# Gated mix of attention and a spectral filter on one core: values as weights of four heads, part of the exponentials as bit patterns on two other engines, folded transforms, an order planned ahead

## The chip, the cores and the metric

One core of a Trainium2 chip runs the kernel. The time is the device time of one execution in microseconds (us); a version's time is the median of its runs. Engines: PE (TensorE: matmuls; PEld is its weight load), DVE (VectorE), ACT (ScalarE), POOL (GpSimd), SP (SyncE, which here issues nearly all DMAs). Each engine works through its own row of instructions in order and waits on semaphores for the others.

## The reference

`x` is 1 x 2048 x 448. A gate of one number per token mixes two branches: softmax attention with 16 heads of width 28, and a filter in the two-dimensional Fourier domain.

```python
g = sigmoid((x * gate_w).sum(-1, keepdims=True))
q, k, v = split(x @ wqkv)                     # 16 heads, Dh = 28
p = softmax(einsum("bhqd,bhkd->bhqk", q, k) * Dh ** -0.5)
a = heads_joined(einsum("bhqk,bhkd->bhqd", p, v)) @ wo
b = irfft2(rfft2(x) * (w_r + 1j * w_i))       # over tokens and features
return g * a + (1 - g) * b
```

There are 16 x 2048 x 2048 exponentials, 1024 blocks of 128 keys by 512 queries of one head.

## The kernel before, in words

*Set-up.* `phase_setup` loads the tokens (`xtok`) and transposes them on PE into `xT`. `proj_setup` and `proj_matmuls` build, for up to four heads at a time, `qTa` and `kTa`: 32 rows for each head, 28 of them data and one a norm that keeps the exponent in range (`proj_knorm` and the bias function behind it: squares, sums by a matmul, a maximum, a DMA that puts the row in place). `vproj_and_gate` makes the values `vsb` (28 columns and a column of ones) and the gate.

*Main loop.* `main_loop_group` goes over six groups: one head by itself, then five groups of three heads. For each block of 512 queries and each of 16 blocks of 128 keys it issues three score matmuls into three PSUM banks (`psS`, two such tiles; each head uses its own 32 rows of the array, so that three run side by side), one exponential on ACT over all three banks (128 x 1536, L557), and 12 value matmuls (L562): there the exponential `Pt` is the weight, in pieces of 128 x 128, and `vsb` (29 columns) streams past it. The result has queries on partitions; DVE divides it by the column of sums (L568, L571).

*Background.* The projections of later heads and the transforms are issued at a low priority between the steps; a scheduler orders all engines by that. They share one PSUM bank (`ps_bg`). The transforms are `fft_f1` (over features), `fft_f2` (over tokens, 128 points), `fft_f34` (transposes, 16-point step with twiddles, product with the filter), `fft_f5` and `fft_f678` (the way back, ending in `bm_sb`, already multiplied by 1 - g). The `tail` transposes each token block of the attention result, multiplies by `wo` and adds `bm_sb`.

Of the kernel before, what the change touches and what calls it, by code (L numbers as in the profile page):

```python
# [12 lines left out]
F32 = mybir.dt.float32  # L13
ACT = mybir.ActivationFunctionType
# [3 lines left out]
BG_PRIORITY_BASE = 10_000_000  # L18


def bcast_last(ap: bass.AP, n: int) -> bass.AP:
    assert ap.ap[-1][1] == 1
    new_ap = [list(p) for p in ap.ap[:-1]] + [[0, n]]
    return bass.AP(tensor=ap.tensor, offset=ap.offset, ap=new_ap)


def strided_rows(t_ap: bass.AP, row0: int, stride: int, count: int) -> bass.AP:
    pstep = t_ap.ap[0][0]
    return _AP(tensor=t_ap.tensor, offset=t_ap.offset + row0 * pstep,
               ap=[[pstep * stride, count]] + [list(x) for x in t_ap.ap[1:]])  # L30


def chunks_of(n: int, c: int):
    return [(i, min(c, n - i)) for i in range(0, n, c)]


def fft_consts(S: int, D: int):
    NT = S // 128
    P = 128
    J = P // NT  # L40
    F = D // 2 + 1
    F2 = 2 * F
    bf16 = ml_dtypes.bfloat16
    fch = chunks_of(F, 128)
    c = {}
    d = np.arange(D)[:, None]
    f = np.arange(F)[None, :]
    Bd = np.concatenate([np.cos(2 * np.pi * d * f / D), -np.sin(2 * np.pi * d * f / D)], axis=1)
    dch = chunks_of(D, 128)
    Bd_pad = np.zeros((len(dch) * 128, F2))  # L50
    Bd_pad[:D] = Bd
    c["Bd"] = np.ascontiguousarray(Bd_pad.reshape(len(dch), 128, F2).transpose(1, 0, 2))
    pp = np.arange(P)[:, None]
    bb = np.arange(P)[None, :]
    Ec = np.cos(2 * np.pi * pp * bb / P)
    Es = np.sin(2 * np.pi * pp * bb / P)
    def perm(M):
        return np.ascontiguousarray(M.reshape(P, J, NT).transpose(0, 2, 1).reshape(P, P))
    R = np.zeros((P, 4, 256))
    R[:, 0, :] = np.concatenate([perm(Ec), perm(-Es)], axis=1)  # L60
    R[:, 1, :] = np.concatenate([perm(Es), perm(Ec)], axis=1)
    R[:, 2, :] = np.concatenate([perm(Ec), perm(Es)], axis=1)
    R[:, 3, :] = np.concatenate([perm(-Es), perm(Ec)], axis=1)
    c["R"] = R
    CS = np.zeros((NT, P, 3, P))
    tt = np.arange(NT)[:, None]
    aa = np.arange(NT)[None, :]
    for g in range(NT):
        for j in range(J):
            b = g + NT * j  # L70
            th = 2 * np.pi * (tt * aa / NT + tt * b / S)
            CS[g, j::J, 0, j::J] = np.cos(th)
            CS[g, j::J, 1, j::J] = np.sin(th)
            CS[g, j::J, 2, j::J] = -np.sin(th)
    c["CS"] = CS
    RB = np.zeros((NT, P, 2, 2 * P))
    for g2 in range(NT):
        for j2 in range(J):
            bh = g2 + NT * j2
            ps = 2 * np.pi * (tt * aa / NT + tt * bh / S)  # L80
            RB[g2, j2::J, 0, j2:P:J] = np.cos(ps)
            RB[g2, j2::J, 0, P + j2::J] = np.sin(ps)
            RB[g2, j2::J, 1, j2:P:J] = -np.sin(ps)
            RB[g2, j2::J, 1, P + j2::J] = np.cos(ps)
    c["RB"] = RB
    mm = np.arange(D)[None, :]
    ff = np.arange(F)[:, None]
    cfac = np.full((F, 1), 2.0)
    cfac[0, 0] = 1.0
    cfac[F - 1, 0] = 1.0  # L90
    Br = cfac * np.cos(2 * np.pi * ff * mm / D) / (S * D)
    Bi = -cfac * np.sin(2 * np.pi * ff * mm / D) / (S * D)
    Binv = np.zeros((P, 2 * len(fch), D))
    qi = 0
    for B in (Br, Bi):
        for (fs, fn) in fch:
            Binv[:fn, qi, :] = B[fs:fs + fn, :]
            qi += 1
    c["Binv"] = Binv
    return {k: v.astype(np.float32).astype(bf16) for k, v in c.items()}  # L100


class Kernel:
    def __init__(self, tc, A_x, A_wqkv, A_wo, B_w_r, B_w_i, gate_w, out):
        self.tc = tc
        nc = self.nc = tc.nc
        self.A_x, self.A_wqkv, self.A_wo = A_x, A_wqkv, A_wo
        self.B_w_r, self.B_w_i, self.gate_w, self.out_ap = B_w_r, B_w_i, gate_w, out
        self.H = H = 16
        self.S = S = A_x.shape[1]  # L110
        self.D = D = A_x.shape[2]
        self.Dh = Dh = D // H
        self.SCALE = float(Dh) ** -0.5
        self.NT = NT = S // 128
        self.P = P = 128
        self.J = P // NT
        self.F = F = D // 2 + 1
        self.F2 = 2 * F
        self.dch = chunks_of(D, 128)
        self.NDC = len(self.dch)  # L120
        self.fch = chunks_of(F, 128)
        self.QW = 512
        assert Dh + 1 <= 32 and S % 512 == 0 and P % NT == 0 and NT <= P and H % 4 == 0
        self.x = A_x[0]
        self.outv = out[0].rearrange("(p t) d -> p t d", t=NT)
        self.tiles = [[(s, 4 * T + s) for s in range(4)] for T in range(H // 4)]
        lastT = len(self.tiles) - 1
        hl = H - 1
        self.tiles[lastT] = [(s, h) for (s, h) in self.tiles[lastT] if h != hl]
        self.tiles.append([(0, hl)])  # L130
        self.repT = len(self.tiles) - 1
        self.head_loc = {}
        for T, ent in enumerate(self.tiles[:-1]):
            for s, h in ent:
                self.head_loc[h] = (T, s)
        groups = [("rep", hl)]
        others = [h for h in range(H) if h != hl]
        for i in range(0, len(others), 3):
            groups.append(("tri", others[i:i + 3]))
        self.groups = groups  # L140
        self.NG = len(groups)
        self._bgcount = 0
        self._bg_saved = None
        self._evac_cnt = 0

    def bg_begin(self):
        assert self._bg_saved is None
        self._bg_saved = self.tc.cur_priority
        self.tc.cur_priority = BG_PRIORITY_BASE + self._bgcount

    def bg_end(self):
        assert self._bg_saved is not None
        self._bgcount = self.tc.cur_priority - BG_PRIORITY_BASE
        self.tc.cur_priority = self._bg_saved
        self._bg_saved = None

    def setup_pools(self, ctx):
        tc = self.tc
        self.per = ctx.enter_context(tc.tile_pool(name="per", bufs=1))
        self.rot2 = ctx.enter_context(tc.tile_pool(name="rot2", bufs=2))  # L160
        self.rot3 = ctx.enter_context(tc.tile_pool(name="rot3", bufs=3))
        self.ps = ctx.enter_context(tc.tile_pool(name="ps", bufs=2, space=bass.MemoryType.PSUM))

    def ps_S(self, shape, dt, name):
        return self.ps.tile(shape, dt, name=name, tag="psS", bufs=2)

    def ps_pv(self, shape, dt, name):
        return self.ps.tile(shape, dt, name=name, tag="pv", bufs=1)

    def ps_bg(self, shape, dt, name):  # L170
        return self.ps.tile(shape, dt, name=name, tag="bg", bufs=1)

    def evac2(self, o, i):
        if self._evac_cnt % 2 == 0:
            self.nc.vector.tensor_copy(out=o, in_=i)
        else:
            self.nc.scalar.copy(out=o, in_=i)
        self._evac_cnt += 1

    def build(self):  # L180
        with ExitStack() as ctx:
            self.setup_pools(ctx)
            self.phase_setup()
            self.fft_setup()
            NTL = len(self.tiles)
            self.qTt = [None] * NTL
            self.kTt = [None] * NTL
            def full_proj(Tlist):
                for T in Tlist:
                    self.proj_setup(T)  # L190
                for which in ("q", "k"):
                    for T in Tlist:
                        self.proj_matmuls(T, which)
                for T in Tlist:
                    self.proj_knorm(T)
                for T in Tlist:
                    self.proj_qbias(T)
            full_proj([self.repT, 0])
            self.vproj_and_gate()
            bg_items = [("proj", T) for T in range(1, NTL - 1)]  # L200
            bg_items += [("fft", f) for f in
                         [self.fft_f1, self.fft_f2, self.fft_f34, self.fft_f5, self.fft_f678]]
            npj = NTL - 2
            plan = {0: [0, npj], 1: [1, npj + 1], 2: [2, npj + 2], 3: [npj + 3], 4: [npj + 4]}
# [99 lines left out]
    def proj_setup(self, T):  # L304
# [4 lines left out]
        if not hasattr(self, "Waug"):  # L309
            self.Waug = {}  # L310
            self._wc = 0
# [489 lines left out]
```

## Time and profile before

| | us |
|---|---|
| median of 2 runs (584.65 to 585.45) | 585.05 |
| span of the profiled execution | 564.9 |
| PE busy in it | 508.8 |
| ACT busy in it | 490.0 |
| DVE busy in it | 213.8 |
| POOL busy in it | 20.8 |

The page gives the span of the profiled execution, from its first to its last instruction, and no other time of its own for it. The two runs lie 20.2 us above that span: what lies around the instructions. PE's busy time is modelled and takes in waiting inside the pipeline, so a busy PE isn't PE at its peak. The granted clock of PE is given in every window; 1.00 is full speed.

### The profile page before, as it was taken

To read this page: it belongs to the slowest core of one execution; us is meant where nothing else is said; L and a number is where in the kernel's file an instruction comes from. 1 tells how busy PE (TensorE), PEld (TensorE's weight loads), DVE (VectorE), ACT (ScalarE), POOL (GpSimd) and SP (SyncE) were. 2 spreads that over 40 slices of the span, in tenths; PEclk is the share of its full clock that TensorE was granted. 3 is DMA by queue.
4 is the path that set the end of the run, shared out by engine and by line. 5 is a ranking of instruction groups with operands and counts; after the bars stand their busy time and mean duration, and the time that the engine had idled before them with its cause. 6 is when DMAs were issued, how large, how long until landed. Compare 5 with 4: busy or idle time off the path is not lost.

```text
span 564.9 us, 13975 instructions
## 1 busy us (share of the span) xinstructions
PE 508.8 (90%) x6088; PEld 256.5 (45%) x6088; DVE 213.8 (38%) x633; ACT 490.0 (87%) x392; POOL 20.8 (4%) x92
## 2 busy tenths in 40 slices
PE   2979988999998899999899999999998998899986
PEld 2424432444443355544355555555544554445541
DVE  4573323322223533322556555333233233333343
ACT  2153986999999899999899999999999999999961
POOL 6240010000000000000000000000000000000000
PEclk9989985699999575799575555757799589999996
DMA  7300000000000000000012221000000000000111
GB/s 252 126 19 20 2 2 1 2 1 2 2 1 2 3 1 1 1 3 1 1 33 54 55 55 26 1 2 1 20 21 20 21 20 20 21 1 27 34 34 41
DMA packets 13947, 13.45 MB, mean 24 GB/s; under 512 B 6191, under 2 KB 12783, under 8 KB 13758
## 3 DMA queue, kind: packets, MB, share of 16 engines
q1 hardware_dynamic: 13886, 12.57, 7.8%
q8 instruction: 47, 0.77, 0.6%
q14 instruction: 14, 0.11, 0.1%
HBM read 10.14 MB, written 1.84 MB: 21 GB/s over the span
## 4 chain that ended last, share of the span: by engine, by line
ACT 48%; PE 39%; issue 7%; DVE 3%; DMA 1%; SPq 0%; ACTq 0%
ACT Pt L557 48%; PE psS L553 12%; PE psPV L562 9%; PE pv L290 2%; PE pqk L353 2%; PE psT L641 2%; DMA Wqkv_sb<-in_A_wqkv_dram 1%; PE psY L714 1%; PE pf_s L747 1%; PE ptx L257 1%; PE psB L662 1%; PE psA L623 1%; PE psZ L705 1%; DVE fin L749 1%; PE psB L664 1%
## 5 line engine op out<-in xcount | busy, mean ns | idle before, releaser
L557 ACT ACTIVATE Pt<-psS 128x1536 bf16<-128x1536 f32 (+1 forms) x352 | 469.4, 1460 | 19.4 <-PE psS L553 10.2
L562 PEld LDWEIGHTS <-Pt 128*128 128x128 bf16 x4096 | 142.3, 100 | 131.1 <-ACT Pt L557 109.6
L562 PE MATMUL psPV<-vsb,Pt 128*128 128x29 bf16 x4096 | 167.1, 182 | 25.3 <-ACT Pt L557 20.8
L553 PE MATMUL psS<-qTa_2343,kTa_2344 32*128 32x512 bf16 x256 | 69.3, 507 | 0.5 <-ACT Pt L557 0.5
L553 PE MATMUL psS<-qTa_950,kTa_951 32*128 32x512 bf16 x256 | 68.8, 530 | 0.4 <-ACT Pt L557 0.4
L553 PE MATMUL psS<-qTa_249,kTa_250 32*128 32x512 bf16 x256 | 60.6, 439 | 1.8 <-ACT Pt L557 1.8
L553 PE MATMUL psS<-qTa_3760,kTa_3761 32*128 32x512 bf16 x192 | 26.5, 384 | 0.5 <-ACT Pt L557 0.4
L718 DVE TENSOR_SCALAR bm_sb<-psY,omg 128x448 bf16<-128x448 f32 x16 | 10.9, 683 | 36.8 <-PE psY L714 36.8
L667 DVE CAST Xri<-psB 128x225 bf16<-128x225 f32 x16 | 6.3, 396 | 25.7 <-PE psB L665 25.7
L749 DVE SCALAR_TENSOR_TENSOR fin<-pf,gsb,bm_sb 128x448 bf16<-128x448 f32 x12 | 8.2, 684 | 20.7 <-PE pf L747 20.7
L257 PE MATMUL ptx<-ident,xtok 128*128 128x128 bf16 (+1 forms) x64 | 6.7, 287 | 10.3 <-DMA xtok<-in_A_x_dram 7.7
L553 PEld LDWEIGHTS <-kTa_250 32*128 32x128 bf16 x256 | 12.8, 93 | 6.4 <-issue 2.3
L747 PE MATMUL pf<-Wo_sb,oTt 128*128 128x448 bf16 (+1 forms) x48 | 14.8, 374 | 0.7 <-DVE oTt L740 0.7
L553 PE MATMUL psS<-qTa_207,kTa_208 32*128 32x512 bf16 x64 | 14.4, 420 | 0.6 <-ACT Pt L557 0.5
L553 PEld LDWEIGHTS <-kTa_951 32*128 32x128 bf16 x256 | 13.0, 97 | 4.1 <-issue 1.8
L553 PEld LDWEIGHTS <-kTa_2344 32*128 32x128 bf16 x256 | 13.0, 95 | 3.6 <-issue 1.2
L571 DVE TENSOR_TENSOR osb<-psPV,recip 128x112 bf16<-128x112 f32 x64 | 13.6, 266 | 0.6
L290 PE MATMUL pv<-Wqkv_sb,xT 128*128 128x449 bf16 x64 | 13.5, 372 | 0.0
L603 DVE CAST V_5523<-psA 97x256 bf16<-97x256 f32 x16 | 6.8, 424 | 16.4 <-PE psA L625 16.4
L603 DVE CAST U_192<-psA 128x256 bf16<-128x256 f32 x16 | 6.8, 425 | 15.7 <-PE psA L625 15.7
L623 PE MATMUL psA<-R_sb,X_sb 128*128 128x256 bf16 (+1 forms) x32 | 12.2, 383 | 0.0
L623 PE MATMUL psA<-R_sb,G_sb 128*128 128x256 bf16 (+1 forms) x32 | 12.2, 382 | 0.0
(484 smaller groups left out, 541.6 us busy)
## 6 DMA issues: line engine op xcount, KB each, us to landing
RBg<-cRB SPq DMA_DIRECT2D x16, 128.0 KB, 2.0
xtok<-in_A_x_dram SPq DMA_DIRECT2D x1, 1792.0 KB
out_dram<-fin SPq DMA_DIRECT2D x16, 112.0 KB, 1.7
CSg<-cCS SPq DMA_DIRECT2D x16, 96.0 KB, 1.8
Wqkv_sb<-in_A_wqkv_dram SPq DMA_DIRECT2D x3, 336.0 KB, 7.4
Wg<-in_B_w_r_dram SPq DMA_DIRECT2D x16, 56.2 KB, 1.8
Wg<-in_B_w_i_dram SPq DMA_DIRECT2D x16, 56.2 KB, 2.0
Bd_sb<-cBd SPq DMA_DIRECT2D x1, 450.0 KB, 3.8
```

Source lines behind the costliest of these rows:

```text
L257: nc.tensor.transpose(out=pt[0:dsz, k, :], in_=self.xtok[:, t, d0:d0 + dsz], identity=self.ident[:])
L290: nc.tensor.matmul(pv[:, e, 0:D + 1], lhsT=self.xT[:, c, 128 * t:128 * t + 128], rhs=self.Wqkv_sb[:, c, 2 * D:3 * D + 1], start=(c == 0), ...
L353: nc.tensor.matmul(pqk[0:M, e, :], lhsT=Wg[:, c, 0:M], rhs=self.xT[:, c, 512 * b:512 * b + 512], start=(c == 0), stop=(c == NDC - 1))
L553: nc.tensor.matmul(psS[:, e, :], lhsT=kTa[32 * s:32 * s + 32, 128 * i:128 * i + 128], rhs=qTa[32 * s:32 * s + 32, qs:qs + QW], start=True, ...
L557: nc.scalar.activation(out=Pt[:, 0:ne, :], in_=psS[:, 0:ne, :], func=ACT.Exp, scale=self.SCALE)
L562: nc.tensor.matmul(psPV[:, e, j, 0:Dh + 1], lhsT=Pt[:, e, 128 * j:128 * j + 128], rhs=self.vsb[:, i, h, 0:Dh + 1], start=first, stop=last)
L571: nc.vector.tensor_tensor(out=self.osb[:, t0:t0 + NQT, h * Dh:(h + 1) * Dh], in0=psPV[:, e, :, 0:Dh], in1=bcast_last(recip[:, e, :, 0:1], Dh),
L603: self.nc.vector.tensor_copy(out=o, in_=i)
L623: nc.tensor.matmul(ps[0:fn, :], lhsT=data_sb[:, t, fs:fs + fn], rhs=Rr, start=True, stop=False)
L641: nc.tensor.transpose(out=psT[:, ri * 256 + fs:ri * 256 + fs + fn], in_=U_tiles[fb][0:fn, ri, g, :], identity=self.ident[0:fn, 0:fn])
L747: nc.tensor.matmul(pf[:, 0:D], lhsT=oTt[0:dsz, c, :], rhs=self.Wo_sb[0:dsz, c, :], start=(c == 0), stop=(c == NDC - 1))
L749: nc.vector.scalar_tensor_tensor(out=fin[:], in0=pf[:, 0:D], scalar=self.gsb[:, t:t + 1], in1=self.bm_sb[:, t, :], op0=ALU.mult, op1=ALU.add)
```

## The change

The kernel is written anew; only the arithmetic of the reference is common. Part by part:

*Values as weights.* `Wp` pads each head to 32 columns, so four heads stand in 128 rows of `qT` and `kT`. The values `V` (32 columns for each head: 28 data, one weight, three zeros) are now the weight of a matmul and 512 exponentials stream past it. The four heads use the four groups of 32 columns of the array and write the four 32-row parts of one bank `pv`. A chunk is four heads by 512 queries: 16 chunks instead of the 21 of before.

*Exponentials in three places.* `stream` takes the 1024 blocks in steps. In each of 360 steps two blocks go to ACT (128 x 1024, `PA`), and in 304 of them a third goes to DVE: scores are scaled so that a score plus a constant, clamped at zero and written as a 16-bit integer, is the bit pattern of a bf16 number near the exponential. GpSimd makes two shifted copies of the pattern (two blocks at once where it can), and PE adds all three copies with weights `W2` and `W3` in the values `V[1]`, `V[2]`: such a block costs three value matmuls, one on ACT costs one.

```diff
+nc.scalar.activation(out=s_ap[:, 0:len(pk)], in_=bank[:, 0:len(pk), :], func=ACT.Exp, scale=LN2 / 128.0)
...
+nc.vector.tensor_scalar(out=tl[:, 0, e, :], in0=self.single[b][:], scalar1=C2, scalar2=0.0,
+                        op0=ALU.add, op1=ALU.max)
...
+for j, sh in ((1, N2), (2, N3)):
+    nc.gpsimd.tensor_scalar(out=t[:, j, 0:n, :], in0=t[:, 0, 0:n, :], scalar1=float(sh), scalar2=1.0,
+                            op0=ALU.add, op1=ALU.mult)
...
+def score(self, out, g, c, i, h):
+    r = slice(32 * h, 32 * h + 30)
+    self.mm(out, self.kT[g % 2][r, 128 * i:128 * i + 128], self.qT[self.chunks.index((g, c)) % 3][r, :],
+            pos=(32 * h, 0))
...
+self.mm(self.pv[32 * h:32 * h + 32, :], self.V[g % 2][e["j"]][:, i, h, :], e["ap"],
+        start=f, stop=False, pos=(0, 32 * h))
-nc.scalar.activation(out=Pt[:, 0:ne, :], in_=psS[:, 0:ne, :], func=ACT.Exp, scale=self.SCALE)
...
-nc.tensor.matmul(psPV[:, e, j, 0:Dh + 1], lhsT=Pt[:, e, 128 * j:128 * j + 128],
-                 rhs=self.vsb[:, i, h, 0:Dh + 1], start=first, stop=last)
```

*Division.* `normalise` copies `pv` (DVE), sends the four rows of sums through DRAM and back in another layout (DMAs on SP), takes reciprocals times the gate, spreads them through DRAM to 32 rows each, and multiplies: `oT`, already transposed. The last chunk does it on DVE alone with 32 x 32 transposes. The output then needs no transpose and no gate.

*Folded transforms.* `e_f1_pe` takes features d and 448 - d together (`xr` is the mirrored copy, made by GpSimd), `e_f2_pe` uses cosine and sine halves, `e_f3_pe` and `e_f3_t` do twiddles and filter, `e_f5_pe` and `e_f6_pe` go back; the last step over tokens and the factor 1 - g (`Rg`, `Rn`) are matmuls that add into the same bank as `oT @ wo` (`e_o_pe`). The filter comes in 16 groups of frequencies, each with 18 DMAs (16 of them rows of `w_r` and `w_i`).

```diff
+def e_f3_t(self, b, bg, r):
+    o = (self.T1, self.T2)[r][bg % 2]
+    self.nc.vector.tensor_tensor(out=o[:], in0=b[:, 0:450].rearrange("p (r f) -> p r f", r=2),
+                                 in1=bc_at(self.Wf[bg % 2][:, r, :], 1, 2), op=ALU.mult)
...
+def e_o_pe(self, b, t):
+    for g in range(4):
+        self.mm(b[:, 0:448], self.oT[:, g, 128 * t:128 * t + 128], self.Wo[:, g, :], start=g == 0, stop=False)
+    self.mm(b[:, 0:225], rp, eo[:, 0:225], start=False, stop=False)
...
```

*Order.* A `Planner` places every task on its engine by assumed durations and writes all rows in that order, with no scheduler behind it (`tc.manual_schedule()`). Scores wait for one of two ACT banks (`pair`) or three single banks (`single`, shared with all background work); value matmuls are taken in groups of up to eight. Two of its rules:

```diff
+n_dve = 310
+unit(f"F2_{bg}", t0, [("PE", 0.55, self.e_f2_pe, (bg,)), ("DVE", 0.56, self.e_f2_ev, (bg,))],
```

PE's row before, late in the main loop, at the end of one value group, one step of scores, and a piece of transform:

```order
L562 LDWEIGHTS Pt_6371
L562 MATMUL psPV_6240<-vsb_172,Pt_6371 128x29
L553 LDWEIGHTS kTa2_2344
L553 MATMUL psS_6403<-qTa2_2343,kTa2_2344 128x512
L553 LDWEIGHTS kTa2_2344
L553 MATMUL psS_6403<-qTa2_2343,kTa2_2344 128x512
L553 LDWEIGHTS kTa2_2344
L553 MATMUL psS_6403<-qTa2_2343,kTa2_2344 128x512
L705 LDWEIGHTS VT_6934
L705 MATMUL psZ_6948<-RBg_6932,VT_6934 97x256
```

Exponentials (`Pt`) were weights and 29 columns streamed. PE's row now, in a chunk of the second group of heads (`PA` and `PD` are exponentials of ACT and DVE, `pair` and `one` score banks):

```order
L328 LDWEIGHTS V1_0_77
L328 MATMUL pv_145<-PD0_136,V1_0_77 32x512
L328 LDWEIGHTS V1_0_77
L328 MATMUL pv_145<-PA1_130,V1_0_77 32x512
L328 LDWEIGHTS V1_0_77
L328 MATMUL pv_145<-PA1_130,V1_0_77 32x512
L328 LDWEIGHTS kT1_73
L328 MATMUL pair0_140<-qT1_70,kT1_73 128x512
L328 LDWEIGHTS kT1_73
L328 MATMUL pair0_140<-qT1_70,kT1_73 128x512
L328 LDWEIGHTS kT1_73
L328 MATMUL one2_144<-qT1_70,kT1_73 128x512
```

The values are the weight, 512 columns stream, and PE goes from column tiles to row tiles with each step. Over the whole program PE has 291 runs of score matmuls, 218 runs of value matmuls and 133 runs of matmuls over the full array.

DVE's row before, in the filter stage of the transforms:

```order
L667 CAST Xri_4178<-psB_4173 128x225
L668 CAST Xri_4178<-psB_4173 128x225
L673 TENSOR_TENSOR cm_t1_4181<-Xri_4178,Wg_4162 128x225
L674 TENSOR_TENSOR cm_t2_4182<-Xri_4178,Wg_4162 128x225
L678 TENSOR_TENSOR cm_t1_4186<-Xri_4178,Wg_4162 128x225
```

Now, in the same stage, DVE's row holds patterns (`PD`) at nearly every second place, between transforms (`Z`), the division (`oT`) and the gate (`xr`):

```order
L903 TENSOR_SCALAR PD3_139<-one0_142 128x512
L903 TENSOR_SCALAR PD3_139<-one1_143 128x512
L660 TENSOR_TENSOR xr_64<-one2_144,cR_85 128x512
L903 TENSOR_SCALAR PD0_136<-one0_142 128x512
L903 TENSOR_SCALAR PD0_136<-one1_143 128x512
L903 TENSOR_SCALAR PD1_137<-one0_142 128x512
L742 CAST Z_81<-one1_143 113x64x8
L903 TENSOR_SCALAR PD1_137<-one0_142 128x512
```

A late transform or division now stands in front of the patterns on DVE, and the patterns in front of GpSimd's copies and PE's value matmuls.

More of the change, by code (lines that the diff above doesn't have):

```diff
@@ L6 @@
 from concourse.bass_types import AP as _AP
-from concourse.masks import make_identity
 import concourse.tile as tile
-from concourse import bass_utils
 from concourse._compat import with_exitstack
@@ new lines, with __init__, placed, done @@
+class Task:
+    __slots__ = ("eng", "dur", "fn", "deps", "start", "end", "done", "seq", "land", "key", "mode", "placed", "then", "port")
+    def __init__(self, eng, dur, fn, deps=(), land=0.0, key=0.0, mode=None, then=None, port=False):
+        self.eng, self.dur, self.fn, self.deps = eng, dur, fn, [d for d in deps if d is not None]
+        self.land, self.key, self.mode, self.then, self.port = land, key, mode, then, port
+        self.placed = False
+class Unit:
+    def __init__(self, name, target, phases, deps=(), bank=True):
+        self.name, self.target, self.phases, self.deps, self.bank = name, target, phases, list(deps), bank
+        self.tasks = []
+        self.opened = False
+    @property
+    def placed(self):
+        return self.opened and len(self.tasks) == len(self.phases) and self.tasks[-1].placed
+    @property
+    def done(self):
+        return max(t.done for t in self.tasks)
+    @property
+    def eng(self):
+        return self.tasks[-1].eng
@@ L768 @@
 ):
[L769 to L770 removed]
+    with tc.manual_schedule():
+        Kernel(ctx, tc, A_x, A_wqkv, A_wo, B_w_r, B_w_i, gate_w, out).build()
 _INS = ['A_x', 'A_wqkv', 'A_wo', 'B_x', 'B_w_r', 'B_w_i', 'gate_w']
```

1647 lines of the change are left out of this document (956 added, 691 removed).

## The prediction

> **What bounds the kernel now.** I read the page first: busy times, granted clock, and the chain that ended last.
>
> ```profile
> PE 508.8 (90%) x6088; PEld 256.5 (45%) x6088; DVE 213.8 (38%) x633; ACT 490.0 (87%) x392; POOL 20.8 (4%) x92
> PEclk9989985699999575799575555757799589999996
> ACT 48%; PE 39%; issue 7%; DVE 3%; DMA 1%; SPq 0%; ACTq 0%
> ```
>
> ACT and PE share the chain; DVE and POOL have room. The clock row has stretches at half speed. Then busy times by windows of 40 us (columns: length, PE, PEld, DVE, ACT, POOL with counts, granted clock, DMA share, GB/s), and the groups by shape.
>
> ```profile
> 140.00:180.00 40.00, 36.96 (x500) 17.21 (x497) 8.74 (x16) 40.00 (x31) 0.00 (x0) 1.00 0.01 2
> 180.00:220.00 40.00, 35.94 (x434) 17.96 (x433) 17.69 (x40) 35.90 (x27) 0.00 (x0) 0.64 0.01 2
> 300.00:340.00 40.00, 39.04 (x486) 22.90 (x486) 23.09 (x108) 37.56 (x28) 0.00 (x0) 0.50 0.23 55
> L557 ACT ACTIVATE Pt<-psS 128x1536 bf16<-128x1536 f32 x336 | 460.2, 1500 | 16.4 <-PE psPV L562 7.9 <-PE psS L553 7.5 <-PE pn_3826 L493 0.4
> L557 ACT ACTIVATE Pt<-psS 128x512 bf16<-128x512 f32 x16 | 9.6, 609 | 2.9 <-PE psS L553 2.7 <-PE psPV L562 0.2
> L562 PE MATMUL psPV<-vsb,Pt 128*128 128x29 bf16 x4096 | 167.1, 182 | 25.3 <-ACT Pt L557 20.8
> L562 PEld LDWEIGHTS <-Pt 128*128 128x128 bf16 x4096 | 142.3, 100 | 131.1 <-ACT Pt L557 109.6 <-issue 6.9 <-DVE osb L571 3.8
> ```
>
> In the main loop ACT is busy for all 40 us of a quiet window and 35.90 where background work crowds PE and DVE: the exponentials bound the middle, and mixing in work costs the bounding engine 10.25% there. Outside the middle:
>
> ```profile
> PE ptx L257 <- DMA xtok<-in_A_x_dram: 7.7, 1, 7.7
> 56.81 4.13 ACT L557 ACTIVATE Pt<-psS 128x1536 bf16<-128x1536 f32 x3 [0.23 <-PE psS L553]
> 543.77 1.61 ACT Pt L557
> 559.70 1.78 PE pf_s L747 x4
> ```
>
> The first exponential starts at 56.8 us, the last ends near 545, the span at 564.9: 78 us lie outside the loop.
>
> **The change, part by part.** One third of the blocks leaves ACT, so I price all engines and look for the longest.
>
> *ACT.* Pitch, not duration, counts, because rows overlap:
>
> ```profile
> 80.66 1.11 ACT L557 ACTIVATE Pt<-psS 128x512 bf16<-128x512 f32 x2 [0.23 <-PE psPV L562]
> 511.64 6.87 ACT L557 ACTIVATE Pt<-psS 128x1536 bf16<-128x1536 f32 x5
> ```
>
> Five of 1536 in 6.87 with a last one of 1.50 give (6.87 - 1.50)/4 = 1.34 us; two of 512 give 1.11 - 0.60 = 0.51. Between them 0.81 ns an element, so 1024 elements take 0.925. ACT has 360 of these (333 us) and 34 of 512 (squares of the projections, output copies: 17): with a few small ones 351 us, where it had 490.
>
> *PE.* Prices at full clock:
>
> ```profile
> 21.60 2.76 PE L353 MATMUL pqk<-xT,WaugQ_209 128*128 128x512 bf16 x12
> 47.77 7.59 PE L290 MATMUL pv<-Wqkv_sb,xT 128*128 128x449 bf16 x39
> 512.24 0.39 PE L553 MATMUL psS<-qTa_3760,kTa_3761 32*128 32x512 bf16 x3
> 512.57 0.66 PE L747 MATMUL pf<-Wo_sb,oTt 128*128 128x448 bf16 x2
> ```
>
> Twelve matmuls of 512 columns: (2.76 - 0.38)/11 = 0.216 us each. Thirty-nine of 449: (7.59 - 0.37)/38 = 0.190. So 0.413 ns a column and 4.6 ns a matmul. Three score matmuls side by side start at 512.24 and the next work at 512.57: 0.33, of which 0.216 is one turn and 0.11 the change to other tiles.
>
> - Scores: 1024 still, each in its 32 rows. In the program they make 355 turns (a turn is one matmul in each row group that has one) in 291 runs: 355 x 0.216 + 291 x 0.11 = 109 us.
> - Values: 4096 weight loads with 29 columns go; 1632 matmuls of 512 columns come (720 blocks once, 304 blocks three times). The trace shows no column tiles. Bound below: four at once, as the score rows run three at once, with the program's unevenness 543 turns in 218 runs: 543 x 0.216 + 218 x 0.11 = 141. Bound above: one after another, 1636 x 0.216 + 24 = 377. I take 141, because the score row is the same array split the other way and shows full overlap.
> - Full array (projections, values, transforms, output): 1145 matmuls, 260,896 columns, 133 runs: 5.3 + 107.7 + 14.6 = 128. The folding is in this count; the transposes of the old transforms and of the old tail are gone.
>
> PE: 378 us. This is the longest row, though its busy time of before can't be set against it, since that takes in waiting.
>
> *DVE.* Start to start of a 512-column read from PSUM:
>
> ```profile
> 56.27 0.69 DVE L478 CAST qTa_950<-pqk_952 128x512 bf16<-128x512 f32 x1
> 56.88 0.16 DVE L298 TENSOR_SCALAR ge<-ge 128x16 f32<-128x16 f32 x1
> ```
>
> 0.61 us. DVE has 496 instructions of about this size (304 patterns, 192 for projections, values, transforms, division, output): 303 us; 22 of 1024 elements at some 0.65 and 90 small ones at 0.15 add 28: 331 us, 54% more than before, but under PE.
>
> *GpSimd.* It gets 296 shifts of 1024 elements and 16 of 512; no such instruction is in the trace. The nearest rows:
>
> ```profile
> L458 POOL COPY WaugK_905<-Wqkv_sb 128x28 bf16<-128x28 bf16 x12 | 2.0, 208 | 0.1
> masks.py:199 POOL TENSOR_SCALAR_AFFINE_SELECT ident<-ident 128x128 bf16<-128x128 bf16 x1 | 0.3, 292 | 0.1
> L265 POOL MEMSET xT<- 64x2048 bf16 x1 | 1.8, 1804 | 0.1
> L316 POOL MEMSET WaugQ_209<- 128x512 bf16 x1 | 0.5, 534 | 0.0
> ```
>
> The two that read and write 16-bit data give (292 - 208)/100 = 0.84 ns an element, so 1.05 us for 1024 and 0.61 for 512: 320 us. If the fixed part is the memsets' (534 less 512 at their slope of 0.83 ns, 0.11 us), AFFINE_SELECT says (292 - 110)/128 = 1.42 ns and the sum is 296 x 1.56 + 16 x 0.84 = 475. I take 320, since copy and select share the way an instruction reads. Trainium skill, "GPSIMD Engine Reference", 3.1: 1.03 cycles an element for at most two operations, 1.8 in the tight loops measured there; at the 1.2 GHz it gives, I estimate 0.86 or 1.5 ns. The first agrees with 0.84, the second is near 1.42; no run here shows which holds for integers.
>
> *SP.* Issue and landing:
>
> ```profile
> 320.10 0.33 SPq L655 DMA_DIRECT2D CSg<-cCS  x1
> 44.19 0.65 SPq L421 DMA_DIRECT2D qTa_249<-brow  x1
> Wg<-in_B_w_r_dram SPq DMA_DIRECT2D x16, 56.2 KB, 1.8
> ```
>
> SP goes from some 100 DMAs to 440: 288 for the filter groups, 105 for 15 divisions, 47 others; at 0.33 us 145 us. I cost it at nothing: a division has the length of a chunk (some 25 us) before its buffer is needed, against four hops of 1.8 and their issue; a filter group has a second buffer. If that cover is gone, DVE stands in front of the filter product, with the patterns queued behind it, then GpSimd's copies, then PE's value matmuls: rival D.
>
> **Sum.** PE starts behind the tokens (7.7 us before) and has little work in the chain of square, norm and copy of the first projection (0.5 + 0.6 us each, a few links): 12 us. Projection, gate and norms of later heads run inside the loop, so the 56.8 us go. After the last value matmul come five DVE instructions, four output blocks in a pipeline of copy and 1.8 us store: 10 us, half of before. In the middle PE, DVE, ACT and GpSimd all have 85 to 100% of PE's load and hand blocks over through two ACT banks, three shared banks and four pattern buffers; the bounding engine then loses what ACT lost in 180 to 220 us, so 378/0.8975 = 421. Span 12 + 421 + 10 = 443. The runs lie 20.2 us over the profiled span (585.05 against 564.9), so 463 us.
>
> **The rivals.**
>
> *A, the column tiles don't run at once* (slower). Value matmuls one after another: PE 614, /0.8975 = 684, with 22 and 20 it is 726 us. It decides from the point where PE's sum is (585 - 42) x 0.8975 = 487, the value term 250, which is fewer than 1.56 of four at once (1632 x 0.216/226). For it: no row shows column tiles. Against it: the score row.
>
> *F, they overlap in part.* A value turn costs 0.27 instead of 0.216, halfway to the 0.33 of a score turn with its change: 543 x 0.27 + 24 = 171, PE 408, 455 + 42 = 497 us. For it: eight matmuls read eight different streams of exponentials, where score rows share a width of 32. Trainium skill, "TensorE: Matmul & The Clock Gate", Part 3, gives three column tiles of 512 columns a gain of 2.38, not 3, which would be 117/0.79 = 148 for the turns, by my estimate the same as 543 x 0.27; no run here shows it yet.
>
> *B, half clock.* The trace shows when it falls and rises:
>
> ```profile
> 36.00:40.00 4.00, 3.24 (x9) 0.65 (x9) 3.17 (x5) 1.06 (x2) 2.34 (x12) 0.65 0.00 0
> 40.00:44.00 4.00, 4.00 (x11) 0.86 (x10) 0.34 (x3) 3.53 (x4) 0.00 (x0) 0.50 0.01 1
> 44.00:48.00 4.00, 4.00 (x23) 2.01 (x22) 1.62 (x2) 0.38 (x2) 0.00 (x0) 0.99 0.33 70
> ```
>
> It falls after a gap in PE's work and returns with dense matmuls; in 300 to 340 us it stayed at 0.50 with short waits in between. At the mean of before, 0.805, the streaming part of PE's sum (898 turns and 113 us, 307) becomes 381, the sum 452, and the time 504 + 42 = 546 us. Under 0.74 it would be slower than before. Against it: PE is nearly full now, and the quiet loop held 1.00 with less work.
>
> *C, GpSimd bounds.* At 1.42 ns: 475, with some 25 us before its first copies and 15 behind its last 515, and 535 us; at the same loss as PE more, about 555. For it: the memset reading above.
>
> *D, a late filter takes the place of the wait on exponentials.* If each of 16 groups comes half its issue time (18 x 0.33/2 = 3.0 us) late: 48 us, 511 us. For it: SP's row is in order and divisions stand between the groups. The same price covers other handovers that are worse than 10%.
>
> *E, no loss.* PE without gaps: 378 + 22 + 20 = 420 us; ACT's own floor is 351 + 42 = 393.
>
> That the change doesn't do what it says is excluded by the counts of its rows: 304 of 1024 blocks leave ACT, 30%.
>
> **Chances.** Forecast (435 to 485) 0.47, A 0.05, F 0.09, B 0.13, C 0.08, D 0.08, E 0.10. The predicted time is the forecast's, 463. The range 418 to 552 takes in E, F, D and most of B, and leaves out A, most of C and the upper end of B, under 0.2. A measurement of this kernel tells about 2% from no change. A and the low end of B's clocks are slower, 0.06; C with more loss or B near its turning point could come within 2%, 0.03; the rest is faster, 0.91.
>
> **What would show it.** The scores: three at once at a pitch of 0.33. The value groups: eight matmuls in 0.54 us (right), 0.65 (F) or 1.7 (A). GpSimd's shift of 1024: 1.05 us or 1.6. ACT busy 351, first exponential before 20 us. Clock above 0.9. DVE waiting on DMAs before T would show D. The prediction is wrong if PE isn't the longest row, or if its gaps in the middle are far from 10%.

## The result, and the profile after

The kernel became slower: 644.66 us (642.72 to 646.60, 2 runs) against 585.05, a ratio of 1.101 (95%: 1.093 to 1.110). Forecast were 463 us. The runs of the kernel before fall in two groups, 562 to 574 and 581 to 588 us; 585.05 is of the longer group, and the ratios of the experiments below are to the shorter one. The profiled execution took 646.6 us, its span is 644.8, that of the kernel before was 564.9. First the page of the kernel after: busy times, granted clock and DMA packets.

```profile
PE 459.6 (71%) x3809; PEld 176.3 (27%) x3809; DVE 347.4 (54%) x592; ACT 369.6 (57%) x402; POOL 330.9 (51%) x331
PEclk8889778795958798795878977659987979697897
DMA packets 86903, 18.00 MB, mean 28 GB/s; under 512 B 75942, under 2 KB 84360, under 8 KB 86852
```

No engine is the bound: the longest row is busy for 71% of the span, where PE and ACT had 90% and 87%. So the question is what all of them wait for. Groups by shape (busy time, mean ns, then the idle time ahead of them and its cause):

```profile
L805 ACT ACTIVATE PA<-pair 128x1024 bf16<-128x1024 f32 x352 | 338.4, 1035 | 171.7 <-PE one L328 134.8 <-PE pair L328 30.9 <-remote 3.5
L824 POOL TENSOR_SCALAR PD<-PD 128x1024 int16<-128x1024 int16 x296 | 310.0, 1047 | 285.6 <-DVE PD L903 213.8 <-PE one L328 34.5 <-PE pair L328 11.7
```

ACT waits for PE, and GpSimd for DVE's patterns. The waits view (total, times, longest) has what DVE and PE wait for, and SP's own row:

```profile
DVE oT L1166 <- DMA Rb<-dr: 133.1, 15, 13.8
PE one L328 <- DVE PD L903: 69.5, 12, 13.6
DVE rec L1154 <- DMA sums<-dr: 38.5, 8, 7.3
...
SPq L331 <- DMA dr<-rec: 141.9, 13, 11.7
```

`Rb`, `sums` and `rec` are the division's: sums of the exponentials through DRAM, their reciprocals back through DRAM. One division in the timeline (start, length; in brackets the idle time ahead and what ended it):

```profile
472.16 0.39 SPq L331 DMA_DIRECT2D dr<-rec  x1
...
484.17 1.71 SPq L331 DMA_DIRECT2D Rb<-dr  x4
...
487.57 0.69 DVE L1166 TENSOR_TENSOR oT<-oraw,Rb 128x512 bf16<-128x512 f32 x1 [12.02 <-DMA Rb<-dr]
488.18 1.28 DVE L903 TENSOR_SCALAR PD<-one 128x512 int16<-128x512 f32 x2
488.92 0.58 PE L328 MATMUL one<-qT,kT 30*128 30x512 bf16 x1 [11.14 <-DVE PD L903]
...
489.02 1.05 POOL L824 TENSOR_SCALAR PD<-PD 128x1024 int16<-128x1024 int16 x1 [12.07 <-DVE PD L903]
```

SP sends the reciprocals at 472.16. The spread copies `Rb` read the same place in DRAM, so SP holds them until the write has landed, 12.0 us later. DVE has L1166 next in its row and stands for 12.02 us; the patterns behind it don't run, their PSUM banks stay full, PE has no bank for scores, GpSimd no patterns, ACT no scores. The same place by windows of 5 us (PE, PEld, DVE, ACT, POOL busy, granted clock, DMA share):

```profile
480.00:485.00 5.00, 0.00 (x0) 0.00 (x0) 0.00 (x0) 0.00 (x0) 0.00 (x0) 0.75 0.22 14
485.00:490.00 5.00, 1.08 (x11) 0.38 (x13) 2.43 (x5) 0.37 (x1) 0.98 (x1) 0.50 0.20 52
...
500.00:505.00 5.00, 4.50 (x44) 2.07 (x44) 4.49 (x9) 4.95 (x7) 4.64 (x5) 1.00 0.01 2
```

Everything stops, restarts at half clock, and only then reaches the state the forecast was made for: 500 to 505 has PE, DVE, ACT and GpSimd all at 90% or more (DVE at 4.49 of 5) at full clock. Such a wait comes in each of the 15 chunks that divide through DRAM, 8.9 us on average (133.1/15).

### The profile page after: what moved, and what is told of

The parts are those of the page before. It is cut to its first block, busy times and chain, and to the rows that moved or that the text cites. A ratio compares the mean times of both kernels' runs of the same rounds, so it can differ in the third digit from the quotient of the medians.

```text
span 644.8 us, 10372 instructions
## 1 busy us (share of the span) xinstructions
PE 459.6 (71%) x3809; PEld 176.3 (27%) x3809; DVE 347.4 (54%) x592; ACT 369.6 (57%) x402; POOL 330.9 (51%) x331
## 2 busy tenths in 40 slices
DMA packets 86903, 18.00 MB, mean 28 GB/s; under 512 B 75942, under 2 KB 84360, under 8 KB 86852
## 5 line engine op out<-in xcount | busy, mean ns | idle before, releaser
L824 POOL TENSOR_SCALAR PD<-PD 128x1024 int16<-128x1024 int16 (+1 forms) x312 | 319.9, 1025 | 286.9 <-DVE PD L903 213.8
L805 ACT ACTIVATE PA<-pair 128x1024 bf16<-128x1024 f32 x352 | 338.4, 1035 | 171.7 <-PE one L328 134.8
L903 DVE TENSOR_SCALAR PD<-one 128x512 int16<-128x512 f32 x304 | 201.6, 685 | 59.7 <-PE one L328 52.8
L328 PE MATMUL one<-qT,kT 30*128 30x512 bf16 x304 | 126.8, 427 | 57.6 <-DVE PD L903 41.5
L328 PE MATMUL pair<-qT,kT 30*128 30x512 bf16 x720 | 146.7, 420 | 20.8 <-ACT PA L805 9.5
L328 PE MATMUL pv<-PD,V 128*32 128x512 bf16 x912 | 151.0, 428 | 13.5 <-DVE PD L903 10.9
L328 PE MATMUL pv<-PA,V 128*32 128x512 bf16 x704 | 134.7, 422 | 7.8 <-DVE V L626 7.8
L328 PEld LDWEIGHTS <-kT 30*128 30x128 bf16 (+1 forms) x1088 | 39.5, 92 | 178.5 <-issue 167.3
L1166 DVE TENSOR_TENSOR oT<-oraw,Rb 128x512 bf16<-128x512 f32 x15 | 10.4, 692 | 133.1 <-DMA Rb<-dr 133.1
L328 PEld LDWEIGHTS <-V 128*32 128x32 bf16 x1632 | 40.6, 98 | 117.4 <-issue 93.9
L328 PE MATMUL one<-xT,Wp 112*128 112x512 bf16 x128 | 37.5, 422 | 28.5 <-DVE Z L742 20.7
L1154 DVE RECIPROCAL rec<-sums 128x16 f32<-128x16 f32 x15 | 3.7, 248 | 38.6 <-DMA sums<-dr 38.5
L328 PEld LDWEIGHTS <-Wp 112*128 112x128 bf16 x128 | 11.7, 104 | 44.7 <-issue 30.1
```

Of the source, the lines that this page charges most:

```text
L328: self.nc.tensor.matmul(out, lhsT=lhsT, rhs=rhs, start=start, stop=stop, skip_group_check=True, **k)
L805: nc.scalar.activation(out=s_ap[:, 0:len(pk)], in_=bank[:, 0:len(pk), :], func=ACT.Exp, scale=LN2 / 128.0)
L824: nc.gpsimd.tensor_scalar(out=t[:, j, 0:n, :], in0=t[:, 0, 0:n, :], scalar1=float(sh), scalar2=1.0, op0=ALU.add, op1=ALU.mult)
L903: nc.vector.tensor_scalar(out=tl[:, 0, e, :], in0=self.single[b][:], scalar1=C2, scalar2=0.0, op0=ALU.add, op1=ALU.max)
L1154: t3 = P.add("DVE", 0.25, lambda: nc.vector.reciprocal(out=self.rec[i][:], in_=self.sums[i][:]), deps=[t2], key=-1)
L1166: t7 = P.add("DVE", 0.62, lambda: nc.vector.tensor_tensor(out=self.oT[:, g, 512 * c:512 * c + 512], in0=self.oraw[i][:], in1=self.Rb[i][:] ...
```

## The experiments

Each ratio below is to the kernel before, run beside the experiment on the same chip. Four chips were used: one for the division on DVE, the rows, the order alone and all exponentials on ACT; one for both remedies together, the two fillers and the spread transforms; one for 250 and 340 patterns; one for 200 and 150. Across chips I compare ratios. Differences in us to the 644.66 of the changed kernel are across chips as well; they are used because three chips gave 487.0, 487.8 and 487.9 us for versions without hops that differ little.

**The division without DRAM.** The theory: DVE's row, stuck behind the division's DMAs, is the loss. The rival: four engines that hand blocks over through few buffers are the loss, and the stops only fall where they'd be anyway. The last chunk already divided on DVE alone; now all do.

```diff
-        if n == 15:
+        if True:
-        in1=self.gb[:]
+        in1=self.gb[:, 4 * c:4 * c + 4, :]
```

> Edit: every chunk divides as the last one does, on DVE with two 32 x 32 transposes, and no sums go through DRAM (gb then holds the gate of all tokens). Theory W (DVE stands in front of its own patterns while the division's DMAs land: 133.1 + 38.5 us in the trace of the changed kernel, and PE, ACT and GpSimd run dry behind it): these 171 us go, and the half-clock stretches behind each stop with them (about 15 times 2 to 3 us); 15 divisions cost DVE some 0.8 us more each. Span 645 - 171 - 40 + 12 = 446, at least under 490; time 460 to 510. DVE's wait for a DMA before the product with the reciprocal is gone. Rival H (the handovers between PE, DVE and GpSimd are the bound, and DVE waits for the DMAs only in time that would be lost anyway): time over 600, with the same idle time put down to PE or to the patterns.

487.0 us (483.5 to 487.8, 4 runs), ratio 0.864 (0.856 to 0.871). Page, DVE's one wait for a DMA in the division, and windows:

```profile
PE 430.4 (89%) x3797; PEld 176.3 (36%) x3797; DVE 357.8 (74%) x601; ACT 370.8 (76%) x405; POOL 330.1 (68%) x325
PEclk9697969999999999999979889769999999999998
```

```profile
DVE rec L1138 <- DMA gb<-g: 8.0, 1, 8.0
```

```profile
100.00:140.00 40.00, 36.73 (x381) 13.63 (x378) 33.87 (x57) 36.52 (x41) 36.98 (x36) 1.00 0.01 2
...
300.00:340.00 40.00, 36.12 (x310) 17.81 (x306) 30.45 (x54) 25.62 (x30) 18.93 (x19) 0.83 0.17 39
```

The span falls from 644.8 to 486.0, by 159 us; the two waits of DVE had been 171.6. The theory stands: the rival had the time over 600. DVE does one more instruction a chunk (two transposes for a copy; its busy time rises by 10 us) and the time still falls by a quarter. From 100 to 140 us, with nothing in front, PE, DVE, ACT and GpSimd are all busy for 85% or more.

**Large pieces instead of small.** The write of `rec` scatters 128 x 16 numbers: 2048 pieces of 4 bytes. Here sums and reciprocals stand as 16 rows of 128 numbers, so that the write of the reciprocals moves 16 pieces of 512 bytes; the four hops stay. The gate gets the same layout once, by five more DMAs.

```diff
-        self.dma(self.sums[i][:], dr1.rearrange("h (t p) -> p h t", t=4))
+        self.dma(self.s16[i][:], dr1.rearrange("h (t p) -> (h t) p", t=4))
...
-        self.dma(dr2.rearrange("h (t p) -> p h t", t=4), self.rec[i][:])
+        self.dma(dr2.rearrange("h (t p) -> (h t) p", t=4), self.r16[i][:])
```

> Edit: the division keeps its four hops through DRAM, but sums and reciprocals are held as 16 rows of 128 numbers, so that the reciprocals are written in 16 pieces of 512 bytes instead of 2048 pieces of 4 bytes. Theory W with small pieces as its cause (SP waited 141.9 us in 13 places for that write, median 11.7): the write lands like the other DMAs, in about 2 us, and the time comes near that of the version that divides on DVE, 465 to 520. Theory W with the four hops as its cause (issue and landing of each, whatever its pieces): the waits shrink by less than half and the time stays over 560. Rival H: over 600.

527.6 us (525.0 to 530.9), ratio 0.937 (0.928 to 0.947): between the two ranges that I had given, 465 to 520 and over 560. SP's row at one division, then waits of DVE and of SP:

```profile
422.56 0.30 SPq L335 DMA_DIRECT2D dr<-r  x1
423.94 1.69 SPq L335 DMA_DIRECT2D Rb<-dr  x4
```

```profile
DVE r L1161 <- DMA s<-dr: 38.0, 7, 16.1
DVE oT L1173 <- DMA Rb<-dr: 16.0, 5, 5.9
...
SPq L335 <- DMA dr<-r: 13.7, 12, 2.4
```

From write to spread 1.4 us, where it was 12.0. SP now stands 1.1 us on average in front of the spread copies (13.7 in 12 places), where it stood 10.9 (141.9 in 13; the 11.7 that I called the median in my expectation is the longest). DVE's wait in front of `oT` falls from 133.1 to 16.0. The wait for the sums is as long as before (38.0), though these pieces are large too: the pieces don't cause that one. The reciprocals cost DVE more in this layout, 0.94 us a chunk instead of 0.25.

**The order alone.** Same transfers as in the changed kernel; the planner is told 14 us for the landing of the write instead of 2.5, so that it sets L1166 later in DVE's row.

```diff
-                   deps=[t4], land=2.5, key=-1000)
+                   deps=[t4], land=14.0, key=-1000)
```

> Edit: only the order. The planner is told that the write of the reciprocals lands after 14 us instead of 2.5, so the product on DVE is placed some 12 us later; the DMAs are the same. Theory W as a matter of order (what is queued behind the wait decides, not the wait): DVE's 133 us mostly go, time 480 to 540. Rival S (SP's own row is the bound, because a later DMA there waits until the slow write has landed, and the filter's loads come late instead): the wait moves to the filter product on DVE and the time stays over 580.

530.8 us (526.4 to 537.2), ratio 0.937 (0.928 to 0.946), as expected. DVE's and SP's waits:

```profile
DVE oT L1166 <- DMA Rb<-dr: 30.3, 6, 9.8
...
DVE rec L1154 <- DMA sums<-dr: 18.9, 5, 7.8
...
SPq L331 <- DMA dr<-rec: 101.9, 13, 11.5
```

The write is as slow as ever, and SP still stands 101.9 us behind it. Yet DVE's two waits fall from 171.6 to 49.2 and the time by 114 us: most of the loss came from the place of L1166 in DVE's row. 44 us over the version without DRAM are left.

**Both together.** Rows of 512 bytes, and 6 us planned for every hop.

```diff
-                   deps=[ta], land=2.5, key=-1000)
+                   deps=[ta], land=6.0, key=-1000)
```

> The division through DRAM in 16 rows of 512 bytes, as in the run before that did this, and now the planner is told that each of its four hops takes 6 us, where it was told 2.2 to 2.5. Same transfers, same arithmetic, another order. If all that is left of the loss is DVE standing in its row in front of a hop (38.0 us for the sums and 16.0 us for the spread reciprocals, against 527.6 us in all and 487.0 with no hop), the two waits fall under 10 us together and the time is 487 to 500. If the transfers themselves cost something (SP's row, or writes that delay other loads), the waits fall and the time stays above 510.

495.3 us (490.5 to 496.2), ratio 0.864 (0.853 to 0.874), where the version without any hop had 0.864 on another chip. A version without hops on this chip (the spread transforms below) took 487.8, so some 8 us of a cost are left. DVE still stands for the sums. Its wait, then SP's row and DVE's at one place:

```profile
DVE r L1161 <- DMA s<-dr: 23.3, 4, 9.3
```

```profile
290.44 4.69 SPq L335 DMA_DIRECT2D Wf<-in_B_w_i_dram  x8
295.17 0.42 SPq L335 DMA_DIRECT2D s<-dr  x1
...
296.80 0.94 DVE L1161 RECIPROCAL r<-s 16x128 f32<-16x128 f32 x1 [6.34 <-DMA s<-dr]
```

The hop itself takes 1.6 us (295.17 to 296.80). What makes DVE wait is SP's row: the loads of a filter group, 16 DMAs from 286.3 to 295.1, are issued in front of the hop. All four waits for the sums here, and all seven with the rows alone, have either filter loads or the 16 loads of the gate (`gb`) just ahead of the hop in SP's row. The planner reckoned with 0.06 us for one filter load; eight of them took 3.6 to 4.7 us here.

So I had expected the wait too low (under 10), and the time was right. Either remedy alone takes about 115 of the 158 us, both together some 149: they are two ways to restore one cover, and don't add.

**All exponentials on ACT.** With the division on DVE, are the patterns worth it?

```diff
-    n_dve = 310
+    n_dve = 0
```

> Edit: division on DVE as in the first run, and no block goes to DVE and GpSimd: 512 steps of two blocks, all exponentials on ACT, 1024 value matmuls instead of 1632. If the patterns pay once the waits are gone: ACT has 512 x 0.93 + 17 = 493 us and bounds, span about 535, time 540 to 570, slower than the first run by over 40 us. If the handovers of patterns are the bound (rival H): this version is the faster of the two.

607.2 us (602.6 to 619.1), ratio 1.076 (1.061 to 1.090): a miss. ACT should have set the pace with a step of 0.93 us. In the timeline PE did:

```profile
519.89 0.61 PE L328 MATMUL pair<-qT,kT 30*128 30x512 bf16 x2
...
520.43 0.61 PE L328 MATMUL pv<-PA,V 128*32 128x512 bf16 x2
```

```profile
452.00:456.00 4.00, 4.00 (x16) 0.73 (x16) 0.00 (x0) 3.78 (x5) 0.00 (x0) 0.50 0.00 0
```

A run of one turn takes 0.54 instead of 0.32, the step of two runs 1.08, above ACT's 0.93: the clock is at half, although PE was busy for 4.00 of these 4 us. Over the four runs the granted clock was 0.71 to 0.75; the profiled run is the longest of them. Each matmul here works on one 32-row or 32-column part, two of four parts at a time. Two fillers ask whether that is the reason.

**A filler over the whole array, and one over a quarter.** The last experiment, and after the scores of each step (from the 17th) one more matmul of 512 columns that nobody reads; background work keeps to two of the three single banks.

```diff
+                    self.mm(self.single[2][:], self.kT[g % 2][:, 128 * i:128 * i + 128],
+                            self.qT[self.chunks.index((g, c)) % 3][:])
```

The second one has rows and columns 0 to 63 of it.

> Division on DVE and all exponentials on ACT (607.2 us before, clock about 0.74), and from the 17th step on one more matmul a step, over the full array (128 rows, 128 columns, 512 columns of scores streamed), whose result nobody reads. It adds work and takes none away. If the granted clock follows how much of the array works, the clock rises over 0.9, the step (two scores, values, filler: 0.8 us) fits under ACT's 0.93, and the time falls to 500 to 540 although PE does 496 x 0.22 = 109 us more. If the clock falls for gaps in PE's row, or for being busy too long, PE's step at half clock goes from 1.08 to 1.5 us and the time rises to 750 or more.

> The same filler of 512 streamed columns on a quarter of the array (64 rows, 64 columns). If the granted clock follows how much of the array works, it stays near 0.5 and the step goes to 1.08 + 0.43 = 1.5 us: 750 us or more. If it follows how long PE is busy, this run has the clock and the time of the one with the full array.

The whole array: 677.3 us (647.4 to 686.2). A quarter: 786.7 us (748.3 and 825.1). Timelines of the two, in this order:

```profile
520.28 0.39 PE L328 MATMUL pair<-qT,kT 30*128 30x512 bf16 x2
...
520.61 0.39 PE L328 MATMUL one<-qT,kT 128*128 128x512 bf16 x1
...
520.93 0.39 PE L328 MATMUL pv<-PA,V 128*32 128x512 bf16 x2
521.25 0.39 PE L328 MATMUL pair<-qT,kT 30*128 30x512 bf16 x2
```

```profile
521.57 0.60 PE L328 MATMUL pair<-qT,kT 30*128 30x512 bf16 x2
...
522.11 0.63 PE L328 MATMUL one<-qT,kT 64*64 64x512 bf16 x1
...
523.21 0.60 PE L328 MATMUL pair<-qT,kT 30*128 30x512 bf16 x2
```

With the whole array the clock is 1.00 here and 0.957 over the profiled run (647.4 us). With a quarter a step here takes 523.21 - 521.57 = 1.64 us at half clock. But the same run has other stretches in which the same steps run with nothing beside them, and at either clock:

```profile
340.00:360.00 20.00, 20.00 (x63) 4.01 (x62) 0.00 (x0) 12.61 (x13) 0.00 (x0) 0.50 0.00 0
720.00:740.00 20.00, 20.00 (x105) 6.04 (x104) 0.00 (x0) 20.00 (x21) 0.00 (x0) 1.00 0.00 0
```

Its two executions had mean clocks of 0.719 (the profiled one) and 0.818. Counted in pieces of 3.4 us that hold steps alone, the clock was 1.00 in all 71 with the whole array, in 28 of 108 with a quarter, and in 4 of 56 without a filler. So the fillers show less than the theory says. Its rival, that a busy PE is enough for the full clock, falls: PE is busy for 20.00 of 20 us in both stretches. The share of the array has a part in it, by the 71 against the 28, but doesn't decide alone, since one share ran at both clocks. What else does isn't shown. One more rival stays open for the fall of the clock without a filler: there PE waits some 0.2 us a step for ACT while the clock is full (2.59 us of work in 444.25 to 447.66, half clock right behind it), and both fillers take most of that wait away.

The time I expected with the whole array was wrong too (500 to 540): a step with the filler is 521.25 - 520.28 = 0.97, not 0.8, since each change of tile kind costs its 0.1 us and a step now has three. PE is then the bound, and the transforms come on top of it.

**Spreading the transforms.** Division on DVE, the planned end of the transforms at 430 us instead of 350.

```diff
-        T = self.T = 350.0
+        T = self.T = 430.0
```

> Division on DVE (487.0 us), and the transforms are planned to end at 430 instead of 350 us, so that their work is spread over more of the run. If what is left over PE's 430 us busy is the crowding of background work in the first two thirds, the time falls to 470 to 480; if the end is set by the late output blocks behind the transforms, it rises to 490 to 505.

487.8 us (487.2 to 489.6), ratio 0.852 (0.845 to 0.859) beside 0.864 (0.856 to 0.871): neither expectation (470 to 480 or 490 to 505), and no difference that these intervals tell.

**How many patterns.** Division on DVE, `n_dve` 250, 340, and then 200 and 150.

> Division on DVE (487.0 us), and 250 instead of 310 blocks as bit patterns. ACT gets 30 exponentials of 1024 more (30 x 0.93 = 28 us, to about 399 busy), GpSimd loses 60 shifts of 1024 (63 us, to 267), PE loses 120 value matmuls (a quarter of a turn of 0.216 us each, 6 us). If the handovers through DVE and GpSimd set the time (GpSimd has 25% of the chain), it falls to 470 to 480. If the granted clock falls where fewer score and value tiles work side by side, as in the run with all exponentials on ACT, the clock goes under 0.90 and the time rises to 495 to 520.

> Division on DVE, and 340 instead of 310 blocks as bit patterns. ACT loses 15 exponentials (14 us), GpSimd gets 30 shifts (31 us, to 361), PE 60 value matmuls (3 us). If ACT or the clock sets the time, it falls to 475 to 483; if the handovers through GpSimd do, it rises to 492 to 505; within 2% of 487 says that several rows stand equally near the end, and no share of work is left that a number would win.

> Division on DVE, 200 blocks as bit patterns (250 took 480.7 us, 310 took 487.0, none took 607.2). ACT gets 25 exponentials of 1024 more than with 250: about 391 + 25 x 0.93 = 414 us busy. If ACT's row is next behind GpSimd's, the time is 485 to 500, at a clock above 0.93. If the clock already falls for want of third score tiles, it goes under 0.90 and the time over 510.

> Division on DVE, 150 blocks as bit patterns. ACT about 391 + 50 x 0.93 = 437 us busy. If ACT's row alone sets the time: 500 to 520 at a clock above 0.93. If the granted clock follows how much of the array works, it falls between that of 250 blocks (0.943) and that of none (0.71 to 0.75): 0.80 to 0.90, and the time is 530 to 570.

Medians of 4 runs each: 250 took 480.7 us (479.7 to 481.3; 0.842 of the shortest run of the kernel before beside it), 200 took 467.7 (467.2 to 469.5; ratio 0.822, 0.817 to 0.826), 150 took 489.3 (489.1 to 490.1; ratio 0.859, 0.857 to 0.861). With 200 and 150 both came out faster than all that I had expected (485 to 500, and 500 or more). The run with 340 took 487.9, and tells nothing: the planner's other rules let only 296 patterns in, as many as with 310 (298). The version with 200 is the fastest of all, 18% faster than before by its ratio. Its page (busy times, clock, the chain by engine), and a window:

```profile
PE 425.6 (91%) x3601; PEld 167.1 (36%) x3601; DVE 293.9 (63%) x503; ACT 411.4 (88%) x454; POOL 227.0 (49%) x229
PEclk9598987999999999999999999999999999999956
PE 38%; ACT 34%; DVE 10%; issue 9%; DMA 4%; SPq 2%; POOL 2%; DVEq 0%; ACTq 0%; POOLq 0%
```

```profile
300.00:340.00 40.00, 37.71 (x331) 14.46 (x324) 31.44 (x52) 38.46 (x42) 21.76 (x22) 1.00 0.10 23
```

GpSimd has gone from 25% of the chain (298 patterns) to 2%, and the stretch 300 to 340, which had 0.83 clock and 25.62 us of ACT, now has 1.00 and 38.46. With 150 ACT has most of the chain (41%, and 433.8 us busy), and the clock, which I had expected at 0.80 to 0.90 if it followed the array, stayed at 0.954. So patterns in a third of the steps (150 of 437, each with a third score tile and three value matmuls) go with a clock that holds, and none with one that doesn't.

## Why the prediction was wrong

The step that failed is SP's: "I cost it at nothing: a division has the length of a chunk (some 25 us) before its buffer is needed, against four hops of 1.8 and their issue". It failed in three places. The write of the reciprocals isn't a hop of 1.8 us: in pieces of 4 bytes SP stood behind it for 10.9 us on average. I took the landing from a load of long rows and looked at the count of DMAs, not at the size of their pieces, though the rearrangement stands in the code. Their issue isn't free either: filter loads stand in front of the division's hops in SP's row, at some 0.45 us each instead of 0.33. And when the buffer is needed doesn't matter; what matters is where the planner set L1166 in DVE's row. It did so by an assumed landing of 2.5 us, so DVE reached it too soon and stood there for 8.9 us on average, fifteen times. The order alone brings 114 us, the pieces alone 117, the division without DRAM 158. Trainium skill, "DMA: Bandwidth & Descriptors", Rules for kernel authors: a strided last dimension becomes one descriptor for each element and should be rearranged. The trace agrees: 86903 packets, 28086 with the rows, and 12.0 against 1.4 us; I had not weighed it.

Rival D named the mechanism (DVE in front of a product that waits for DMAs, patterns behind, then GpSimd, then PE) and put it in the wrong place, at the filter, with a size of 48 us. Measured were 133.1 + 38.5 us of waits at the division, 11.4 a chunk, and the half clock after nearly every stop. The filter's products are no line of the waits.

*The 20.2 us around the span* were wrong as well. The profiled runs here lie 1.8 to 2.1 us over their own spans (646.6 and 644.8; with the division on DVE 487.8 and 486.0). So the profile of before must have come from another, shorter run than the two timed ones, of about 567 us by that term. By the right term the sum would have been 443 + 1.8 = 445. Two slips carry no weight in the sum: what lies outside the loop of before is 76 us (56.8, and 545.4 to 564.9), not 78, and the value matmuls are 1632, not the 1636 of rival A's bound.

*The rest of the sum*, read where the division doesn't stand in the way. In the run with the division on DVE:

```profile
13.82 1.57 DVE L387 COPY Wp<-Z 112x448 bf16<-112x448 bf16 x2 [10.45 <-DMA Z<-in_A_wqkv_dram]
...
22.19 1.02 ACT L805 ACTIVATE oT<-pair 128x1024 bf16<-128x1024 f32 x1 [0.38 <-PE pair L328]
...
103.21 0.39 PE L328 MATMUL pair<-qT,kT 30*128 30x512 bf16 x2
...
103.53 0.39 PE L328 MATMUL pv<-PD,V 128*32 128x512 bf16 x1
...
109.01 0.39 PE L328 MATMUL pv<-PD,V 128*32 128x512 bf16 x2 [0.20 <-POOL PD L824]
...
109.02 0.58 PE L328 MATMUL pv<-PA,V 128*32 128x512 bf16 x2
...
109.78 0.39 PE L328 MATMUL pair<-qT,kT 30*128 30x512 bf16 x2
...
473.29 0.61 PE L328 MATMUL pv<-PA,V 128*32 128x512 bf16 x6
```

- Head: 22.2 us, not 12. DVE pads the weights only when they have landed, at 13.8; I had counted the tokens' 7.7 and not the weights. Tail: 486.0 - 473.9 = 12.1, not 10.
- Scores: pitch 0.32 (103.21 to 103.53), forecast 0.33.
- Values: column tiles do run at once, as forecast. Eight matmuls in three turns from 109.01 to 109.78 are 0.77; 3 x 0.216 + 0.11 = 0.76. Rivals A and F fall. Trainium skill, "TensorE: Matmul & The Clock Gate", Part 3, gives column tiles less than their number; this stream shows no such loss.
- GpSimd: 1.047 us for 1024, forecast 1.05. C falls in its price. Still GpSimd had 25% of the chain, since a pattern block comes back through two shifts in one row: a bound by order, as I read it, that a busy time doesn't show.
- DVE: a pair of patterns of 1.28 and one of 0.69 give a pitch of 0.6, as forecast; busy 347.4 against 331. ACT: 369.6 against 351; 338.4/352 = 0.96 us for one of 1024, where I had taken 0.925.
- The middle: 473.9 - 22.2 = 452 us, not 421: 378 us of PE with a loss of 16%, not 10.25%. The quiet windows bear the forecast out (36.73 us of PE in 40). Where projections and transforms come in, PE waits in between (0.83 and 0.93 us at 309 and 310 us) and the clock falls, to 0.83 in 300 to 340; that this crowding is the cause isn't shown, since spreading the transforms changed nothing. The 10.25% was a loss of ACT in one window of before, and I applied it to all. With 200 patterns the middle is 430.
- Rival B: half clock came, as a consequence of the stops, and in the run with ACT alone by itself. My reading of it, that it "falls after a gap in PE's work and returns with dense matmuls", was too simple; the row that I quoted (40 to 44 us: PE 4.00 busy, clock 0.50) spoke against it.

So without the stops the design comes to 487.0 us with the change's own number of patterns and to 467.7 with the best one, against 463; the kernel as changed doesn't: the division's way through DRAM, fifteen times, turned a gain into a loss of 10%. That the forecast comes so near them is partly luck: the term around the span was 18 us too high, the head and the tail 12 us too low, the middle up to 31.

What stays open: what the wait for the sums costs in time by itself. That SP's other loads cause it is read from its row; no run moved them. And what makes the clock fall and come back, beyond a busy PE.

## What to carry to other kernels

In an order that is planned by assumed durations, check the one assumed for each transfer against its smallest contiguous piece, check the time that the issuing engine needs for each (0.06 us assumed, 0.45 measured), and ask what is queued behind the instruction that consumes it: a slow transfer costs its time on every engine if the consumer stands in the row that feeds the others. Where the data is small and an engine in the path has room, do the exchange there (one more DVE instruction a chunk beat four hops). When work is split over engines by a number, move that number last, after the stops are gone: here the best value tried was 200, not 310, a ratio of 0.822 instead of 0.864.

## What the runs showed of the hardware

A busy PE is not enough for the full clock. With two of four tiles in each matmul turn it sat at 0.50 through a stretch in which PE was busy for 4.00 of 4 us. One more matmul a step over the whole array brought 0.957 over the run. With one over a quarter of the array the same steps ran at 0.50 in 340 to 360 us and at 1.00 in 720 to 740, PE busy for all of both. So how much of the array works has a part in it, and isn't the whole rule. Trainium skill, "TensorE: Matmul & The Clock Gate", Part 1, describes a gate that opens after a few us of sustained activity and closes after idle ones; these runs differ from it, if activity is read as a busy PE.

A write to DRAM of 8 KB in 2048 pieces of 4 bytes held SP for 10.9 us on average before a read behind it could go, 8 KB in 16 pieces of 512 bytes for 1.1. To issue the eight loads of half a filter group took SP 3.6 to 4.7 us.
